# Attention and a routed MoE on one core: small VectorE operations taken out or handed to ScalarE, the first expert's weights loaded behind the second routing instead of from a guess

## The chip, the core and the metric

The kernel runs on one core of a Trainium2 chip. Its engines work side by side, each through a queue of its own: TensorE (PE; PEld is its weight load) does matmuls and transposes, VectorE (DVE) and ScalarE (ACT) move results out of PSUM and do elementwise work, GpSimd (POOL) issues gathers and scatters by index, SyncE (SP) issues the other DMAs. The metric is the device time of one execution in microseconds, the median of several runs.

## The reference, cut to what matters

```python
# q, k, v: (8 batches, 8 heads, 576, 64); p: (8, 8, 32, 64)
p_packed = sm_attn(p, k, v)             # 32 packed queries of each head attend to its 576 keys
out = sm_attn(q, p_packed, p_packed)    # 576 queries of each head attend to the 32 packed rows
x = out.transpose(0, 2, 1, 3).reshape(4608, 512)
...
logits = x @ w_gate + modality_bias[modality_id]     # 8 experts
e_idx = np.argmax(logits, axis=1)
gate_w = softmax(logits)[e_idx]
for e in range(8):
    out[e_idx == e] = gate_w * (np.maximum(x[e_idx == e] @ w1[e], 0) @ w2[e])   # 512 -> 1024 -> 512
```

With these inputs the argmax picks three experts only: expert 4 for 2311 rows, expert 5 for 1406, expert 7 for 891. Of the first quarter of the rows (the first routing) 569 go to expert 4 and 583 to expert 5; of the first half 1158, 841 and 305 go to experts 4, 5 and 7.

## The kernel before, in words

**Attention** is cut into eight units: a pair of batches (four pairs) and one of two groups of heads. A unit loads k, q and v, transposes them on TensorE (ScalarE copies `kT` out of PSUM, L218), and makes the scores of the packed queries. `scores1` finds the row maximum on VectorE (L239), turns it into the bias `nb` (L242), and ScalarE takes the exponential with that bias and the scale (L246). `a` and `p` steps multiply by v and give the packed rows; then `g`, `s` steps make the second softmax, on VectorE but for the exponential (L316 to L338, `a2T`). `x` steps (L354) multiply by the packed values: one matmul gives the outputs and, in extra columns, the gate logits. ScalarE copies the outputs to `xs` (L365), VectorE the logits to `lt` (L367); both read one PSUM tile of a pool of two, so that the next but one tile waits for both. `w` stores `xs` to the scratch in DRAM (SyncE, L379 and L380).

**The loop.** Units 0 to 5 run in one loop of a schedule written by hand: the string `ORDER` lists one period, in which each item is a step of the unit n, or of a later one (`>`). Each engine runs its instructions in the order in which they are issued there. An `e` issues the next piece of the extra work of a unit (`more`: a routing, or the split of W1), an `f` the next scatter (`spread`). The rest of units 6 and 7 follows the loop, and a scheduler mixes it with the first MoE slots.

**Routing.** After units 1, 3, 5 and 7 (`routing(i)`, from L417) VectorE computes from `lt` each row's expert, its rank and its gate weight. `scatter(i)` writes the rows' numbers into a list on DRAM: nine indirect DMAs by GpSimd (L469), each with a cast of its column of indices on VectorE ahead of it (L468). A table of **slots** is made from the counts by some 48 operations on tiles of 128x8 and less (`table_phase`, L577): table a, 2 slots, after the second routing; table b, 4 slots, after the third; table c, the rest, after the last. The argument behind the table's name is the expert that the phase starts with.

**A slot** takes 256 rows of one expert: gather (L662), transpose (L675), first matmul (L695; L714 for half slots), relu, second matmul (L730), scatter of the output (L735). The fp32 product is made of three fp32r ones, so W1 and W2 are split into a high part (ScalarE, L655) and a low part (VectorE, L656) at each change of expert. `load_w` (L644) brings 2 x 1024 KB of W1 or W2.

**The guess.** After the first routing `first_expert` (L535 to L545) finds the expert with most rows so far, SyncE reads it as `e0i`, and W1 of that expert is loaded. `split_first` splits it in the loop's last pieces. Table a starts with that expert; a branch at the first slot (L843) loads and splits W1 again if the table's first slot is of another.

Of the kernel before, what the change touches and what calls it, by code (L numbers as in the profile page):

```python
# [8 lines left out]
F32 = mybir.dt.float32  # L9
# [14 lines left out]
def packed_attn_moe_kernel(  # L24
# [14 lines left out]
    nc = tc.nc  # L39
# [127 lines left out]
    def prep_p(ps1, n4):  # L167
        t = ps1.tile([P, 512], F32, name="ps1")
        for n in range(4):
            nc.tensor.transpose(out=t[:, n * P:n * P + P], in_=pz[:, n4 + n].rearrange("p a d -> p (a d)"),  # L170
                                identity=ident)
        yield
        nc.vector.tensor_copy(out=pT[:, n4:n4 + 4, :], in_=t.rearrange("p (n c) -> p n c", n=4))
        yield
# [10 lines left out]
    def attention(i, g, lt, A, Z):  # L185
# [49 lines left out]
        def scores1(u):  # L235
            s1 = scores(ps2, pT[:, 2 * (2 * i + u) + g, :], D_["k"], u)
            yield
            mx = sm.tile([P, 1], F32, name="mx")
            nc.vector.tensor_reduce(mx, s1, axis=AX.X, op=ALU.max)  # L239
            yield  # L240
            nb = sm.tile([P, 1], F32, name="nb")
            nc.vector.tensor_scalar_mul(nb, mx, -SCALE)  # L242
# [4 lines left out]
                                 scale=SCALE, accum_out=r1[:, u])  # L247
# [94 lines left out]
        def xpart(c0):  # L342
# [24 lines left out]
            nc.vector.tensor_copy(out=lt[:, g, :, c0:c0 + w], in_=xq[:, :, :, P:XW])  # L367
# [24 lines left out]
        for nm, f, args in (("k", trans, [("k", *z) for z in fw]), ("q", trans, [("q", *z) for z in fw]),  # L392
# [3 lines left out]
            for n, z in enumerate(args or [()]):  # L396
# [4 lines left out]
    ORDER = ("<f >>c0 e >>>k4 >t >>>k2 s0 >>c0 >q4 >t >>>k4 >>>k3 e >>dv >q0 >>>k0 >>c0 s0 e >q0 f s0 >>>k2 >>r s0 >s1 "  # L401
# [15 lines left out]
    def routing(i, lt, ps1):  # L417
# [42 lines left out]
        dests[i] = dsf  # L460
# [4 lines left out]
    def scatter(i):  # L465
        for c in range(NC):
            dsi = sm.tile([P, 1], I32, name=f"dsi{c}", bufs=2)
            nc.vector.tensor_copy(out=dsi, in_=dests[i][:, c:c + 1])  # L468
            ins = ins_of(nc.gpsimd.indirect_dma_start(  # L469
                out=lst, out_offset=bass.IndirectOffsetOnAxis(ap=dsi, axis=0),  # L470
# [63 lines left out]

    def first_expert():  # L535
        cnt, mxc = st_("cnt"), st_("mxc", 1)
        tt(out=cnt, in0=base[1], in1=base0, op=ALU.subtract)
        nc.vector.tensor_reduce(mxc, cnt, axis=AX.X, op=ALU.max)
        nc.vector.scalar_tensor_tensor(out=cnt, in0=cnt, scalar=mxc, in1=desc[:, 0, :], op0=ALU.is_equal, op1=ALU.mult)
        e0 = const.tile([P, 1], F32, name="e0")  # L540
        nc.vector.tensor_reduce(e0, cnt, axis=AX.X, op=ALU.max)
        tsc(out=e0, in0=e0, scalar1=-1.0, scalar2=float(E), op0=ALU.mult, op1=ALU.add)
        e0i = const.tile([P, 1], I32, name="e0i")
        nc.vector.tensor_copy(out=e0i, in_=e0)
        return e0, e0i  # L545
# [195 lines left out]
    NU = 2 * NA[1]  # L741
    with ExitStack() as actx:
# [13 lines left out]
        def route(i):  # L756
            yield from routing(i, lts[i], ZL["ps1"])
            if i == 0:
                E0.extend(first_expert())
                E0.append(val(E0[1], 0, 0, (ET.SP,), 0, E - 1))  # L760
                load_w(W, 0, E0[2])
# [10 lines left out]
        def split_first():  # L772
            yield
            yield
            for z in range(4):
                split_w(W, 0, None, (z,))
                yield

        E0 = []
        more = {-1: rest(), NU - 1: split_first()}  # L780
# [5 lines left out]
        with tc.manual_schedule(engines={ET.PE, ET.DVE, ET.Activation, ET.SP}):  # L786
            for n in range(-6, NU + 6):
                for z in ORDER.split():
                    nm = z.lstrip("<>")
                    m = n + z.count(">") - z.count("<")  # L790
                    if nm in "ef":
                        next((more if nm == "e" else spread).get(m, iter(())), None)
# [17 lines left out]
    T = [table_phase("a", E0[0], NA[0], None, SA[0])]  # L810
    er = val(T[0]["tab"], 0, 1, (ET.SP,), 0, E - 1)
    load_w(W, 1, er)
# [24 lines left out]
    def sw(n, which, after=()):  # L837
# [4 lines left out]
        def go():  # L842
            if n == 0 and which == 0:  # L843
# [132 lines left out]
```

## Time and profile before

| | us |
|---|---|
| median of three runs | 632.21 |
| the three runs | 629.63, 632.21, 632.35 |
| the profiled execution: time | 628.84 |
| the profiled execution: span of the trace | 627.0 |
| TensorE busy in the span | 575.3 (92%) |
| VectorE, ScalarE, GpSimd busy | 251.3, 219.6, 148.3 |

The span is what the trace covers; the 1.8 us between the span and the execution's time lie around it. All rows below are of this one execution, which ran 3.4 us under the median. `xs` stores of units 0 to 5 are issued at 51.3, 65.1, 83.2, 99.6, 116.9 and 137.6 us; the loop's last `a2T` is done at 148.3; the first matmul of a slot starts at 162.2 and the last output scatter at 616.9.

### The profile page before, as it was taken

How to read it: one execution, taken by the hardware profiler on the slowest of the kernel's cores; microseconds unless marked ns; L12 is line 12 of the kernel's file. 1: busy time of each engine (PE TensorE's matmuls, PEld its weight loads, DVE VectorE, ACT ScalarE, POOL GpSimd, SP SyncE). 2: the span in 40 equal slices, each digit the busy share in tenths (PEclk: the TensorE clock that was granted, in tenths of full speed). 3: DMA queues.
4: the chain of work that ended last, by engine and by line, in shares of the span. 5: the costliest groups of instructions: out<-in, count | busy, mean ns of one | idle time of the engine just before them, and what ended most of it. 6: DMA issues, size and time to landing. Idle time of an engine off the chain costs nothing. (4 is left out here: it accounts for less than half of the span.)

```text
span 627.0 us, 12550 instructions
## 1 busy us (share of the span) xinstructions
PE 575.3 (92%) x4820; PEld 501.0 (80%) x4820; DVE 251.3 (40%) x669; ACT 219.6 (35%) x401; POOL 148.3 (24%) x183
## 2 busy tenths in 40 slices
PE   4979888875999999999999999999999999999982
PEld 4657666653889889899889889989989989989982
DVE  1469988987564421127120155012012012012281
ACT  3658676852432121126121154112112122122371
POOL 2020031352162142232203121312212112212221
PEclk9989999966899999999999999999999999999997
DMA  9899999939719311025902117211011011011112
GB/s 295 238 269 310 316 359 320 271 80 344 247 34 321 146 37 52 18 70 213 414 30 68 53 52 286 70 52 53 35 52 51 35 52 53 34 52 52 37 51 56
DMA packets 49226, 87.49 MB, mean 140 GB/s; under 512 B 12529, under 2 KB 22321, under 8 KB 49137
## 3 DMA queue, kind: packets, MB, share of 16 engines
q1 hardware_dynamic: 39024, 63.92, 31.9%
q0 software_dynamic: 8528, 22.16, 11.0%
q8 instruction: 49, 0.80, 0.5%
q10 hardware_dynamic: 1584, 0.28, 0.2%
q14 instruction: 41, 0.33, 0.2%
HBM read 66.78 MB, written 19.56 MB: 138 GB/s over the span
## 5 line engine op out<-in xcount | busy, mean ns | idle before, releaser
L695 PE MATMUL ps_h<-x_hl,w1h 128*128 128x256 f32 x1088 | 197.5, 283 | 0.7 <-ACTq L926 0.7
L695 PEld LDWEIGHTS ps_h<-x_hl,w1h 128*128 128x128 f32 x1088 | 170.9, 192 | 2.7 <-ACTq L926 0.9
L695 PE MATMUL ps_h<-x_hl,w1l 128*128 128x256 f32 x544 | 154.2, 283 | 0.0
L700 DVE SCALAR_TENSOR_TENSOR hl<-ps_h,hh 128x512 fp32r<-128x512 f32 x68 | 47.0, 691 | 256.2 <-ACT hh L699 253.8
L730 PE MATMUL ps_o<-w2h,hh 128*128 128x512 f32 x296 | 118.1, 399 | 2.8 <-ACT ot L734 2.0
L730 PE MATMUL ps_o<-w2h,hl 128*128 128x512 f32 x296 | 116.5, 393 | 0.0
L730 PE MATMUL ps_o<-w2l,hh 128*128 128x512 f32 x296 | 115.9, 392 | 0.2 <-DVEq L865 0.2
L695 PEld LDWEIGHTS ps_h<-x_hl,w1l 128*128 128x128 f32 x544 | 104.2, 192 | 0.6 <-issue 0.5
L699 ACT ACTIVATE hh<-ps_h 128x512 fp32r<-128x512 f32 x68 | 40.7, 598 | 160.7 <-PE ps_h L695 149.5
L735 POOL DMA_INDIRECT out_dram<-ot,mt x37 | 40.6, 1096 | 184.2 <-ACT ot L734 120.5
L734 ACT ACTIVATE ot<-ps_o,mt 128x512 f32<-128x512 f32 x37 | 25.4, 688 | 143.7 <-PE ps_o L730 120.0
L730 PEld LDWEIGHTS ps_o<-w2h,hh 128*128 128x128 f32 x296 | 55.7, 188 | 14.3 <-ACT ot L734 3.1
L469 POOL DMA_INDIRECT lst<-meta,dsi x36 | 37.1, 1031 | 126.4 <-DVE dsi L468 68.7
L730 PEld LDWEIGHTS ps_o<-w2h,hl 128*128 128x128 f32 x296 | 55.6, 188 | 11.5
L730 PEld LDWEIGHTS ps_o<-w2l,hh 128*128 128x128 f32 x296 | 55.7, 188 | 11.0 <-DVEq L865 0.6
L662 POOL DMA_INDIRECT xt<-x_scr,mt x46 | 45.0, 979 | 76.1 <-PE ps_t L675 29.7
L218 ACT COPY kT<-ps 128x512 f32<-128x512 f32 (+1 forms) x80 | 40.9, 553 | 21.1 <-PE ps L215 18.1
L354 PE MATMUL ps<-bd,a2T 64*128 64x136 f32 (+1 forms) x320 | 29.1, 339 | 9.8 <-DVE bf L523 4.3
L678 DVE TENSOR_TENSOR x_hl<-ps_t,x_hl 128x512 fp32r<-128x512 f32 x42 | 27.6, 684 | 19.7 <-ACTq L865 13.5
L354 PEld LDWEIGHTS ps<-bd,a2T 64*128 64x128 f32 (+1 forms) x320 | 22.0, 206 | 16.7 <-issue 8.3
L660 POOL DMA_DIRECT2D mt<-lst x23 | 17.3, 752 | 54.9 <-DMA out_dram<-ot,mt 44.4
L215 PE MATMUL ps<-ident,rek 128*128 128x128 f32 x144 | 22.4, 293 | 8.2 <-DMA rek<-in_k_dram 7.6
(187 smaller groups left out, 645.4 us busy)
## 6 DMA issues: line engine op xcount, KB each, us to landing
raw<-in_moe_w_dram SPq DMA_DIRECT2D x24, 1024.0 KB
rek<-in_k_dram SPq DMA_DIRECT2D x16, 576.0 KB
req<-in_q_dram SPq DMA_DIRECT2D x16, 576.0 KB
ld_v<-in_v_dram SPq DMA_DIRECT2D x16, 576.0 KB
x_scr<-xs SPq DMA_DIRECT2D x28, 256.0 KB
x_scr<-ld_v SPq DMA_DIRECT2D x4, 256.0 KB
x_scr<-xs SPq DMA_DIRECT2D x14, 64.0 KB
raw<-in_p_dram SPq DMA_DIRECT2D x2, 384.0 KB
```

Source lines behind the costliest of these rows:

```text
L215: nc.tensor.transpose(out=t[:, c * P:c * P + P], in_=src[:, (f0 + c) * P:(f0 + c) * P + P], identity=ident)
L218: nc.scalar.copy(out=T_[:, f0:f0 + w, :], in_=t[:, :w * P].rearrange("p (f r) -> p f r", f=w))
L354: nc.tensor.matmul(xp[rows, pr, z * XW:z * XW + XW], a2T[rs, t0:t0 + n], D_["bd"][rs, u, :], start=True, stop=True)
L469: ins = ins_of(nc.gpsimd.indirect_dma_start(out=lst, out_offset=bass.IndirectOffsetOnAxis(ap=dsi, axis=0), in_=meta[:, i * NC + c, :], in_ ...
L662: ins.append(nc.gpsimd.indirect_dma_start(out=xt[:, t], out_offset=None, in_=x_scr[0:NA[ph] * 2 * S] if ph < 2 else x_scr, in_offset=bass. ...
L678: iv = tt(out=M["xl"][:, :, ts], in0=ps, in1=M["xh"][:, :, ts].bitcast(F32), op=ALU.subtract)
L695: nc.tensor.matmul(ps[:, f], M[a][:, j, (f0 + f) * P:(f0 + f) * P + P], M[b][:, j], start=(n == 0), stop=(n == 3 * KD - 1))
L699: ia = nc.scalar.activation(out=M["hh"][:, fs], in_=ps, func=AF.Relu)
L700: iv = nc.vector.scalar_tensor_tensor(out=M["hl"][:, fs], in0=ps, scalar=0.0, in1=M["hh"][:, fs].bitcast(F32), op0=ALU.max, op1=ALU.subtract)
L730: nc.tensor.matmul(op, M[a][:, j, t * P:t * P + P], M[b][:, j, :], start=(n == 0), stop=(n == 3 * KF - 1))
L734: nc.scalar.activation(out=ot, in_=op, func=AF.Copy, scale=mt.bitcast(F32)[:, t, 2:3])
L735: nc.gpsimd.indirect_dma_start(out=out, out_offset=bass.IndirectOffsetOnAxis(ap=mt[:, t, 1:2], axis=0), in_=ot, in_offset=None, bounds_che ...
```

## The change

- `pT` is multiplied by the scale when it is copied out of PSUM; `scores1` takes the maximum with the sign turned and writes `nb` at once (16 operations of L242 go), and the exponential has no scale.
- The `lt` copies go from VectorE to ScalarE, right behind the `xs` copy of the same tile.
- The indices of a routing are cast at once, 9 columns, in `routing` (one operation for nine, L468 goes).
- `first_expert` goes, with the load of W1 after the first routing, and with the branch at the first slot. Table a is made within the loop, in one straight piece (`first_phase`, an `e` of unit 5), starting from expert 0; then W1 of the table's own first expert is loaded, and split late in the loop.
- `ORDER` is another string.
- Table b's code stands behind the rest of units 6 and 7; scatters of the loop depend by hand on the VectorE or ScalarE instruction issued just ahead of them.

```diff
-        nc.vector.tensor_copy(out=pT[:, n4:n4 + 4, :], in_=t.rearrange("p (n c) -> p n c", n=4))
+        nc.vector.tensor_scalar_mul(pT[:, n4:n4 + 4, :], t.rearrange("p (n c) -> p n c", n=4), SCALE)
...
-            mx = sm.tile([P, 1], F32, name="mx")
-            nc.vector.tensor_reduce(mx, s1, axis=AX.X, op=ALU.max)
-            yield
             nb = sm.tile([P, 1], F32, name="nb")
-            nc.vector.tensor_scalar_mul(nb, mx, -SCALE)
+            nc.vector.tensor_reduce(nb, s1, axis=AX.X, op=ALU.max, negate=True)
...
-                                 scale=SCALE, accum_out=r1[:, u])
+                                 accum_out=r1[:, u])
...
-            nc.vector.tensor_copy(out=lt[:, g, :, c0:c0 + w], in_=xq[:, :, :, P:XW])
+            nc.scalar.copy(out=lt[:, g, :, c0:c0 + w], in_=xq[:, :, :, P:XW])
...
-        dests[i] = dsf
+        dests[i] = sm.tile([P, NC], I32, name="dsi", bufs=2)
+        nc.vector.tensor_copy(out=dests[i], in_=dsf)
...
-            dsi = sm.tile([P, 1], I32, name=f"dsi{c}", bufs=2)
-            nc.vector.tensor_copy(out=dsi, in_=dests[i][:, c:c + 1])
...
-    def first_expert():
...
+    no_expert = const.tile([P, 1], F32, name="no_expert")
+    nc.vector.memset(no_expert, 0.0)
...
-            if i == 0:
-                E0.extend(first_expert())
-                E0.append(val(E0[1], 0, 0, (ET.SP,), 0, E - 1))
-                load_w(W, 0, E0[2])
...
-        def split_first():
-            yield
-            yield
-            for z in range(4):
-                split_w(W, 0, None, (z,))
-                yield
+        def first_phase():
+            T.append(table_phase("a", no_expert, NA[0], None, SA[0]))
+            yield
+            T[0]["er"] = val(T[0]["tab"], 0, 1, (ET.SP,), 0, E - 1)
+            load_w(W, 0, T[0]["er"])
+            yield
...
-    T = [table_phase("a", E0[0], NA[0], None, SA[0])]
-    er = val(T[0]["tab"], 0, 1, (ET.SP,), 0, E - 1)
-    load_w(W, 1, er)
+    load_w(W, 1, T[0]["er"])
...
-            if n == 0 and which == 0:
-                with tc.If(val(tb, s, 3, IFE, 0, 1) > 0):
-                    load_w(W, 0, val(tb, s, 1, (ET.SP,), 0, E - 1))
-                    split_w(W, 0)
-            else:
-                with ExitStack() as es:
-                    for z in after if n == 0 else ():
-                        es.enter_context(tc.issue_after(z))
-                    split_w(W, which)
+            with ExitStack() as es:
+                for z in after if n == 0 else ():
+                    es.enter_context(tc.issue_after(z))
+                split_w(W, which)
```

**VectorE, table a, before.** The table's operations are dealt out among those of the second softmax (`m`, `st`, `dn`; `ps_1853` is a tile of an `x` step).

```order
L319 TENSOR_REDUCE m_1889<-st 128x18
L551 TENSOR_TENSOR ex_m<-eidx,ex_s 128x8
L566 TENSOR_TENSOR row<-row_e,ex_s 128x8
L568 TENSOR_REDUCE tab_f<-ex_s 128x1
L504 TENSOR_TENSOR dot<-starts,ex_s 128x8
L504 TENSOR_TENSOR dot<-ends,ex_s 128x8
L552 TENSOR_REDUCE tab_f<-ex_m 128x1
L567 TENSOR_REDUCE tab_f<-row 128x1
L499 TENSOR_REDUCE red<-dot 128x1 x2
L367 COPY lt<-ps_1853 128x2x24
L321 TENSOR_TENSOR st<-st,m_1889 128x576
L326 TENSOR_REDUCE dn<-st 128x18
```

**VectorE, table a, after.** It is one piece (the first 12 of its 48 rows), in which most rows read what the row ahead wrote.

```order
L563 TENSOR_TENSOR cnt<-run_84,base_80 128x8
L487 TENSOR_SCALAR tl_f<-cnt 128x8
L488 CAST tl_i<-tl_f 128x8
L489 TENSOR_SCALAR tl_i<-tl_i 128x8
L490 CAST tl_o<-tl_i 128x8
L570 TENSOR_SCALAR cl<-cnt 128x8
L582 MEMSET tab_f 128x1
L509 TENSOR_SCALAR key<-eidx,no_expert 128x8
L582 MEMSET tab_f 128x1
L510 TENSOR_SCALAR key_m<-key 128x8
L511 TENSOR_TENSOR key<-key,key_m 128x8
L517 TENSOR_TENSOR bf<-key 128x64
```

The table has moved out of the softmax of the loop's last units and stands between two softmax pieces.

**SyncE, the load of W1, before.** `raw_114` is W1 as loaded; it stands after the first routing, ahead of the loads of k and q (`rek`, `req`) of later units.

```order
L207 DMA ld_v<-in_v_dram 64x4x576 x2
L631 TENSOR_LOAD e0i
L644 ISA
L644 DMA raw_114<-in_moe_w_dram 128x2x1024
L644 ISA
L644 DMA raw_114<-in_moe_w_dram 128x2x1024
L195 DMA rek<-in_k_dram 128x2x576 x2
L195 DMA req<-in_q_dram 128x2x576 x2
```

**SyncE, after.** The same two loads stand behind those of the last q and ahead of unit 4's `xs` stores; SyncE reads the expert from `tab_a` first.

```order
L207 DMA ld_v<-in_v_dram 64x4x576 x2
L195 DMA req<-in_q_dram 128x2x576 x2
L615 TENSOR_LOAD tab_a
L628 ISA
L628 DMA raw_114<-in_moe_w_dram 128x2x1024
L628 ISA
L628 DMA raw_114<-in_moe_w_dram 128x2x1024
L376 DMA x_scr<-xs 64x4x256 x2
L377 DMA x_scr<-xs 64x256
```

The load has moved past the k, q and v loads of the loop, and past the stores of units 2 and 3, and now waits for table a.

**VectorE behind the loop, before.** Three `lt` copies stand among the end of table b and the next key; `lt<-ps_2471` is the first.

```order
L557 CAST tab_b<-tab_f 128x7
L513 TENSOR_SCALAR key<-eidx,last_b 128x8
L605 SCALAR_TENSOR_TENSOR pref<-pref,tab_f 1x1
L608 CAST pre_b<-pref 1x1
L367 COPY lt<-ps_2471 128x2x24
L514 TENSOR_SCALAR key_m<-key 128x8
L515 TENSOR_TENSOR key<-key,key_m 128x8
L521 TENSOR_TENSOR bf<-key 128x64
L367 COPY lt<-ps_2487 128x2x24
```

**ScalarE behind the loop, after.** The same three copies, each right behind the `xs` copy of its tile.

```order
L362 COPY xs<-ps_2297 128x2x3x128
L364 COPY lt<-ps_2297 128x2x24
L362 COPY xs<-ps_2313 128x2x3x128
L364 COPY lt<-ps_2313 128x2x24
L661 CAST x_hl<-ps_t_2287 128x4x128
L362 COPY xs<-ps_2334 128x2x3x128
L364 COPY lt<-ps_2334 128x2x24
L661 CAST x_hl<-ps_t_2287 128x4x128
L639 CAST w2h<-raw_2236 128x1024 x4
```

The copies left VectorE's queue, where table b stands ahead of them, for ScalarE's.

## Rows read from the trace of the kernel before

**Rows 1.** Busy us by stretch: length, five engines (named in the row), TensorE clock, DMA share, GB/s.
```profile
core 0: us, PE busy (x) PEld busy (x) DVE busy (x) ACT busy (x) POOL busy (x), PEclk, DMA share, GB/s
51.55:65.33 13.78, 13.78 (x242) 10.80 (x240) 12.26 (x31) 11.26 (x24) 0.00 (x0) 1.00 1.06 323
65.33:83.44 18.11, 15.14 (x247) 11.27 (x245) 16.92 (x60) 11.90 (x26) 3.36 (x3) 1.00 1.05 320
83.44:99.92 16.48, 14.61 (x240) 11.01 (x239) 12.77 (x37) 11.16 (x25) 5.76 (x6) 1.00 1.06 351
99.92:121.95 22.03, 19.74 (x324) 14.41 (x323) 21.76 (x101) 16.09 (x35) 5.06 (x5) 1.00 1.03 311
121.95:148.40 26.45, 14.70 (x178) 10.35 (x179) 24.33 (x82) 13.48 (x26) 11.60 (x11) 0.74 0.59 159
148.40:162.20 13.80, 11.56 (x121) 9.16 (x121) 8.19 (x48) 6.82 (x9) 0.00 (x0) 0.51 0.98 361
162.20:616.00 453.80, 448.01 (x2969) 404.73 (x2965) 130.42 (x252) 121.01 (x202) 113.19 (x116) 1.00 0.27 91
```

**Rows 2.** Timeline of SyncE's DMA issues: start us, us, engine, line, operation.
```profile
51.33 1.28 SPq L379 DMA_DIRECT2D x_scr<-xs  x2
...
77.59 0.97 SPq L644 DMA_DIRECT2D raw<-in_moe_w_dram  x2
...
99.55 1.27 SPq L379 DMA_DIRECT2D x_scr<-xs  x2
```

**Rows 3.** Groups of instructions by line, 0 to 165 us: busy, mean ns, idle before.
```profile
L239 DVE TENSOR_REDUCE mx<-ps 128x1 f32<-128x576 f32 x16 | 12.0, 749 | 1.0 <-PE ps L229 1.0
...
L656 DVE TENSOR_TENSOR w1l<-raw,w1h 128x1024 fp32r<-128x1024 f32 x4 | 4.9, 1219 | 0.1
...
L367 DVE COPY lt<-ps 128x48 f32<-128x48 f32 x21 | 4.2, 202 | 8.8 <-ACT xs L365 8.8
L655 ACT CAST w1h<-raw 128x1024 fp32r<-128x1024 f32 x4 | 4.1, 1046 | 0.0
...
L468 DVE CAST dsi<-dsf 128x1 int32<-128x1 f32 x27 | 3.1, 134 | 0.0
...
L242 DVE TENSOR_SCALAR nb<-mx 128x1 f32<-128x1 f32 x16 | 2.2, 139 | 0.1
```

**Rows 4.** Timeline of VectorE: first and last of six operations of `first_expert`.
```profile
75.73 0.11 DVE L537 TENSOR_TENSOR cnt<-run,base 128x8 f32<-128x8 f32 x1
...
76.71 0.15 DVE L544 CAST e0i<-e 128x1 int32<-128x1 f32 x1
```

**Rows 5.** Timeline of VectorE: four of its rows from 108 to 122 us.
```profile
108.63 0.16 DVE L579 TENSOR_TENSOR cnt<-run,base 128x8 f32<-128x8 f32 x1
...
116.50 0.15 DVE L551 TENSOR_TENSOR ex_m<-eidx,ex_s 128x8 f32<-128x8 f32 x1
...
117.14 0.19 DVE L367 COPY lt<-ps 128x48 f32<-128x48 f32 x1
...
121.51 0.15 DVE L557 CAST tab_a<-tab_f 128x7 int32<-128x7 f32 x1
```

**Rows 6.** Timeline of all engines behind the loop.
```profile
148.40 1.73 PE L354 MATMUL ps<-bd,a2T 64*128 64x136 f32 x12 [4.34 <-DVE bf L523]
...
150.22 0.80 ACT L365 COPY xs<-ps 128x768 f32<-128x768 f32 x1 [4.09 <-PE ps L354]
...
151.94 0.18 DVE L367 COPY lt<-ps 128x48 f32<-128x48 f32 x1
...
152.18 2.23 PE L354 MATMUL ps<-bd,a2T 64*128 64x136 f32 x16 [2.04 <-DVE lt L367]
```

**Rows 7.** Waits of TensorE, 162 to 627 us: us in total, times, longest.
```profile
PE ps_h L714 <- DVE w1l L656: 1.7, 1, 1.7
...
PE ps_h L695 <- ACTq L926: 0.7, 1, 0.7
```

**Rows 8.** Timeline of TensorE at 127 us.
```profile
127.34 0.44 PE L292 MATMUL ps<-ident,pd 128*128 128x128 f32 x2 [3.47 <-DVE dsi L468]
```

More of the change, by code (lines that the diff above doesn't have):

```diff
@@ L398, in attention @@
         return steps
-    ORDER = ("<f >>c0 e >>>k4 >t >>>k2 s0 >>c0 >q4 >t >>>k4 >>>k3 e >>dv >q0 >>>k0 >>c0 s0 e >q0 f s0 >>>k2 >>r s0 >s1 "
[3 rows of a table removed]
+    ORDER = (">>c0 >p >q2 s1 >>>k4 >t >>c0 s0 >>>k3 >q3 >>>k2 >t s1 >s0 >>>k4 f >s0 >>c0 >>>k1 x0 >s0 >q3 >>>k2 f >g "
[3 rows of a table added]
     def run_all(u, order):
@@ L466, in scatter @@
         for c in range(NC):
-            dsi = sm.tile([P, 1], I32, name=f"dsi{c}", bufs=2)
-            nc.vector.tensor_copy(out=dsi, in_=dests[i][:, c:c + 1])
             ins = ins_of(nc.gpsimd.indirect_dma_start(
-                out=lst, out_offset=bass.IndirectOffsetOnAxis(ap=dsi, axis=0),
+                out=lst, out_offset=bass.IndirectOffsetOnAxis(ap=dests[i][:, c:c + 1], axis=0),
                 in_=meta[:, i * NC + c, :], in_offset=None))
@@ L533, in sel_at @@
         return o
-    def first_expert():
[L536 to L545, printed above, removed]
     def expert_at(starts, ends, v, out_):
@@ L741, in packed_attn_moe_kernel @@
     NU = 2 * NA[1]
+    T = []
+    no_expert = const.tile([P, 1], F32, name="no_expert")
+    nc.vector.memset(no_expert, 0.0)
     with ExitStack() as actx:
@@ L770, in rest @@
             yield
-        def split_first():
+        def first_phase():
+            T.append(table_phase("a", no_expert, NA[0], None, SA[0]))
             yield
+            T[0]["er"] = val(T[0]["tab"], 0, 1, (ET.SP,), 0, E - 1)
+            load_w(W, 0, T[0]["er"])
             yield
-            for z in range(4):
-                split_w(W, 0, None, (z,))
-                yield
-        E0 = []
-        more = {-1: rest(), NU - 1: split_first()}
+        more = {-1: rest(), NU - 1: first_phase()}
         spread = {}
@@ L790, in packed_attn_moe_kernel @@
                     m = n + z.count(">") - z.count("<")
-                    if nm in "ef":
-                        next((more if nm == "e" else spread).get(m, iter(())), None)
+                    if nm == "e":
+                        next(more.get(m, iter(())), None)
+                    elif nm == "f":
+                        ins = next(spread.get(m, iter(())), None)
+                        if ins is not None:
+                            at = next(z for z in reversed(nc.cur_bb.bb.instructions) if z.engine in (ET.DVE, ET.Activation))
+                            tc.add_manual_dep(ins, at.name, SYNC, reason="scatters with time between them")
                     elif 0 <= m < NU or (m == NU and nm[0] not in "xw") or (m == NU + 1 and nm[0] in "dkcq"):
@@ L882, in packed_attn_moe_kernel @@
         Z1.update(ps1=ZL["ps1"], ps2=ZL["ps2"], xs=ZL["xs"])
-        T.append(table_phase("b", T[0]["last"], NA[1], T[0]["used"], SA[1] - SA[0]))
         ZL["st"] = (lp, zq)
@@ L888, in packed_attn_moe_kernel @@
         run_all(u, "x0 x1 x2 w")
+        T.append(table_phase("b", T[0]["last"], NA[1], T[0]["used"], SA[1] - SA[0]))
         for _ in routing(NA[1], lts[NA[1]], ZL["ps1"]):
```

6 rows, old and new, of the table ORDER are left out of this document.

## The prediction, made before the changed kernel had run

> **What bounds the kernel now.** I read the busy time by stretch first, with the bounds set where unit after unit stores its `xs`. TensorE has 448.01 of the slots' 453.80 us [rows 1]: there it is the bound, with 5.8 us to win at most. So the change has to earn its time ahead of 162 us, in three places that differ.
>
> The stretches of units 0 to 3 (51.55 to 99.92, 48.4 us): the first is all TensorE, 13.78 of 13.78; the second and third issue as many matmuls (242, 247, 240) and take 18.11 and 16.48 [rows 1]. Two things stand over them. The DMA share is above 1 in all three, at 320 to 351 GB/s: the queue of loads is never empty. And in the second VectorE is busy for 16.92 of 18.11. W1's 2 x 1024 KB are issued at 77.59, inside it [rows 2].
>
> The tail of the loop (99.92 to 148.40, 48.5 us): VectorE is busy 21.76 + 24.33 = 46.1 of it, TensorE 34.4 [rows 1]. VectorE is the bound: TensorE waits for it, for example 3.47 us ahead of 127.34 [rows 8]. In the last part the granted clock is .74 on average, and .51 in the 13.8 us behind the loop: TensorE had work for 14.70 of the 26.45 us, the clock fell to the lower of its two levels, 1.2 GHz, for about half of them, and the 11.56 busy us behind the loop run nearly all at that level.
>
> **The change, part by part.** The sum is made against the profiled 628.84.
>
> *Loop, units 0 to 3.* `first_expert` is a chain: its six timed operations start at 75.73 to 76.71 [rows 4], five steps of .196 us where each operation needs the one before it. With the last one's step it held VectorE for 1.05 us in a stretch where that engine is nearly full: −1.1, and 17.0 for the second stretch. The load of W1, 2.1 MB, leaves a queue that is always busy: at 351 to 320 GB/s that is 6.0 to 6.6 us of transfer which the loads behind it no longer wait for. How much of it TensorE gets is unknown. Nothing at one end; at the other all three stretches fall to the first one's 13.78, 41.3 us, which is −7 for both effects. The third stretch has 16.48 − 14.61 = 1.9 us without TensorE; I take 1.4 of it, since steps of VectorE that TensorE waits for stay. Sum of the part: −2.5 (0 to −7).
>
> *Loop, tail.* What VectorE loses: an `lt` copy, 202 ns long [rows 3], between a step of .07 and .20; I take .13, nine times, −1.2. Sixteen of 18 casts of indices: a small operation among others takes a step of .07 (nine, counting the double one as two, between 116.50 and 117.14 [rows 5]; their own 134 ns overlap [rows 3]): −1.1. Four `nb` at .07: −.3. Together −2.6. The maximum with its sign turned I cost as the 749 ns it takes now [rows 3]; no row shows a turned sign, and the same pass over 576 elements is the nearest. The `lt` copies cost ScalarE some .2 each, which lies beside its busy share of 51 to 73% there (16.09 of 22.03, 13.48 of 26.45 [rows 1]); bare, nine would be 1.8.
>
> What VectorE gains is dearer. Table a, dealt out before between 108.63 and 121.51 [rows 5], is one block of 48 rows, of which I count 33 that read what the row ahead wrote. Interleaved, 48 × .07 = 3.4. Straight, 33 × .196 + 15 × .07 = 7.5. So +4.1, and as VectorE bounds the tail, all of it is on the path. The routing's chain loses its partners too: eight of its operations stood among the table's, 8 × (.196 − .07) = +1.0. Then W1: SyncE reads the expert from the finished table, and the load takes 6.0 to 6.6 us beside its .97 of issue [rows 2]. `xs` stores of unit 4 wait behind it on SyncE. ScalarE's `w1h` (4 × 1046 ns) and VectorE's `w1l` (4 × 1219 ns [rows 3]) stand in their queues behind softmax work of the last unit, about 8 us of VectorE by the rows behind the block; I take a wait of 0 for them, at most 2. If it came, everything behind on ScalarE, the last unit's exponentials first, would be late. Part: −2.6 + 4.1 + 1.0 = +2.5 (−2.6, the savings alone, to +7, dependent steps everywhere and the wait).
>
> On dependent operations the Trainium skill speaks against my largest term. "VectorE: DVE Perf Modes", section "The DRAIN you can't avoid", says that a next operation starts only when the pipe is empty, and that a semaphore between operations costs nothing extra; dependent rows would then cost no more than others. By that the block costs +0 and the sum is 4.1 lower. The trace has .07 against .196 per step and does not agree.
>
> *Behind the loop.* TensorE's second `x` tile starts at 152.18, after 2.04 us without work, released by the `lt` copy at 151.94 [rows 6]. ScalarE's copy of `xs` from 150.22 took .80, so it was done at 151.02; the `lt` copy came .92 later because table b stands ahead of it on VectorE. On ScalarE it follows at once. −1.0 (0 to −1.5); the clock does not matter for a wait. Table b itself must still be ready for its slots, which start some 2 slots, over 40 us, later.
>
> *Slots.* Table a starts with expert 0 as its "expert so far", not with a guess; of the three that occur the first is then expert 4 instead of 5 (the largest of the first quarter, 583 rows against 569, so that the guess held and no reload ran). The number of slots stays 20, 17 full and three halves. Before, the last two were halves with a change of expert between, and TensorE waits 1.7 us there for `w1l` [rows 7]. A half gives half the time to hide a split. Now halves are followed by a full slot of another expert twice, as once before, which cost .7 [rows 7], and there is no change ahead of the last slot: −1.7 + .7 = −1.0 (0 to −2). The branch that goes costs a few register instructions before the first slot; I take nothing, as `w2h` was still being cast there.
>
> *Sum.* −2.5 + 2.5 − 1.0 − 1.0 = −2.0, so 626.8 for an execution like the profiled. That one ran 3.4 under the median of the three; the median is what is measured: 632.2 − 2.0 = **630.2**. Half a per cent, 3.2 us, is about what a measurement here can tell from no change: 629.05 and 635.4 are the bounds.
>
> **The rivals.**
>
> *The loop falls to TensorE's floor.* If the loads are what holds the second and third stretch, they go from my 45.9 to 41.3: 4.6 more, 625.6. For it speaks the DMA share above 1; against it that TensorE is not busy to the brim where VectorE is.
>
> *The table's block is no dearer than before.* If dependent rows step as interleaved ones do, the 4.1 is not lost: 626.1. That is what the page named above makes of it. Against it stand the steps of .196.
>
> *Slower: the block starves TensorE and its clock.* While VectorE works through routing and table, both PSUM tiles of the pool of two that the softmax scores use are held; TensorE soon runs out of other work. It idles some 6 us, and the low clock, now granted for part of the last stretch, comes for all of it. The 14.70 us of work at a mean of .74 would take 14.70 × .74 / .5 = 21.8: +7.1, of which the idle time hides up to half: +3.5 to +7.1. With the middle, 5.5, 635.7. It decides when TensorE's idle time in the block exceeds the 3.47 seen now [rows 8]. For it: VectorE has no slack at 46.1 of 48.5. Against: in the new order TensorE has transposes of q to do beside it.
>
> *Nothing is gained in the loop.* ScalarE's `lt` copy may come as late as VectorE's did, and W1 may not have held anyone: without the −2.5 the time is 632.7.
>
> **How the numbers follow.** Forecast .45, its own range 627 to 634, and .13 of it under 629.05. Floor .17 (625.6), block for nothing .09 (626.1), slower .19 (635.7 and above), nothing gained .10 (632.7). Faster: .13 + .17 + .09 = .39. Slower .19. The rest, .42, within half a per cent. The range that leaves out 2 in 10 reaches from 622.5, where floor and a cheap block partly join, to 638, with the slower case's upper end.
>
> **What would show it.** Units' stores: the third after the first (51.33 to 99.55 now [rows 2]) should be 2 to 3 us nearer. The block of 48 table rows on VectorE should take 7 to 8 us, not 3 to 4. No cast of indices should stand among the softmax. TensorE's longest wait in the tail should stay under some 4 us, and the clock's mean near .74. `w1h` should not wait for its load. Behind the loop TensorE should wait for ScalarE's `lt` about 1 us less, and in the slots the single wait of 1.7 should be gone. The prediction is wrong if the last stretch of the loop grows by more than 3 us (clock or W1's landing), or if units 0 to 3 come down to 41 us.

## The result, and the profile after

The changed kernel takes 639.85 us (median of four runs, 638.91 to 641.43) against 631.22 for the kernel before beside it: a ratio of 1.0141, 95% interval 1.0106 to 1.0176. It is slower by 8.6 us, where 2.0 less was forecast. The profiled execution took 640.36, with a span of 638.8.

Busy time by stretch of the changed kernel, with the bounds set at the same events as in [rows 1]: the `xs` stores of units 0, 1, 2, 3 and 5, then the first matmul of a slot.

```profile
core 0: us, PE busy (x) PEld busy (x) DVE busy (x) ACT busy (x) POOL busy (x), PEclk, DMA share, GB/s
54.48:68.96 14.48, 14.48 (x241) 10.04 (x240) 11.83 (x26) 11.56 (x28) 0.00 (x0) 1.00 1.03 300
68.96:87.90 18.94, 16.44 (x244) 11.12 (x243) 15.35 (x41) 11.80 (x29) 4.78 (x5) 0.91 1.04 322
87.90:108.00 20.10, 17.99 (x241) 11.83 (x240) 12.12 (x26) 11.67 (x28) 4.66 (x5) 0.92 0.96 262
108.00:151.34 43.34, 31.38 (x461) 20.59 (x459) 37.62 (x123) 25.24 (x55) 10.72 (x11) 0.84 0.66 183
151.34:173.25 21.91, 16.04 (x155) 12.59 (x151) 16.96 (x83) 11.13 (x22) 5.96 (x5) 0.62 0.98 319
173.25:628.00 454.75, 447.63 (x2969) 404.80 (x2965) 122.46 (x234) 116.31 (x199) 112.18 (x116) 1.00 0.25 84
```

Units 0 to 3 now take 53.5 us (54.48 to 108.00) instead of 48.4. The first two stretches are .7 and .8 longer; the third is 20.10 for 16.48, with the same number of matmuls (241 for 240) and less than 12.2 us of work on each of VectorE and ScalarE. TensorE's time without work is about the same in it (2.1 for 1.9); it counts as busy for 3.4 us more, at a granted clock of .92 for 1.00. From unit 3's stores to the first slot matmul it is 65.3 us; it was 62.3. The slots did not move.

**The third stretch.** Timeline of the changed kernel in it, all engines, some rows left out.

```profile
90.91 0.96 POOL L465 DMA_INDIRECT lst<-meta,dsi  x1 [0.40 <-issue]
...
91.03 0.95 PE L270 MATMUL ps<-ld_v,a1T 64*64 64x128 f32 x11
...
92.17 0.96 POOL L465 DMA_INDIRECT lst<-meta,dsi  x1 [0.30 <-ACT st L320]
...
92.31 0.45 PE L270 MATMUL ps<-ld_v,a1T 64*64 64x128 f32 x3 [0.33 <-issue]
...
93.44 0.95 POOL L465 DMA_INDIRECT lst<-meta,dsi  x1 [0.30 <-issue]
...
94.83 0.42 PE L270 MATMUL ps<-ld_v,a1T 64*64 64x128 f32 x3 [0.52 <-issue]
...
95.67 0.37 ACT L218 COPY kT<-ps 128x256 f32<-128x256 f32 x1 [3.68 <-remote]
```

TensorE does the last matmuls of a step of 24 mostly three at a time, with gaps "<-issue": it waits for nothing that the profile shows. ScalarE stands still for 3.68 us, released by "remote", an event that the records don't place. All of it lies beside four scatters of the list that GpSimd issues in a row: one at 89.29, and the three shown, 1.6 us behind it and then 1.3 us apart. Before, each scatter had its own cast on VectorE ahead of it [rows 3]. Right behind this crawl the granted clock is low, .60 and .54 from 96 to 100 us.

**The tail.** Timeline of the changed kernel from the table's first row to the split of W1.

```profile
127.48 0.16 DVE L563 TENSOR_TENSOR cnt<-run,base 128x8 f32<-128x8 f32 x1
...
130.00 0.17 DVE L522 TENSOR_TENSOR ends<-starts,tl_o 128x8 f32<-128x8 f32 x1
130.20 0.23 DVE L527 TENSOR_SCALAR sel_g<-ends,sidx 128x8 f32<-128x8 f32 x1
...
135.63 0.16 DVE L541 CAST tab_a<-tab_f 128x7 int32<-128x7 f32 x1
135.71 0.75 DVE L239 TENSOR_REDUCE nb<-ps 128x1 f32<-128x576 f32 x1
...
136.51 0.97 SPq L628 DMA_DIRECT2D raw<-in_moe_w_dram  x2
136.55 0.74 ACT L243 ACTIVATE a<-ps,nb 128x576 f32<-128x576 f32 x1 [6.60 <-DVE nb L239]
...
137.43 1.29 PE L229 MATMUL ps<-kT,pT 64*32 64x320 f32 x16 [5.70 <-ACT a L243]
...
144.98 3.89 ACT L639 CAST w1h<-raw 128x1024 fp32r<-128x1024 f32 x4 [3.39 <-DMA raw<-in_moe_w_dram]
...
148.03 1.25 PE L351 MATMUL ps<-bd,a2T 64*128 64x136 f32 x8 [3.42 <-DVE st L313]
```

Table a's 48 rows fill VectorE from 127.48 to 135.71, 8.2 us. The row maximum `nb` stands behind them; ScalarE's exponential waits 6.60 for it, TensorE 5.70. Then the load of W1, issued at 136.51, is there at 144.98: ScalarE, whose next instruction is the split, waits 3.39 for it, and TensorE 3.42 behind that. The granted clock over 108.00 to 151.34 is .84, and .62 up to the first slot.

**Behind the loop**, the `lt` copy follows its `xs` copy at once.

```profile
163.89 0.80 ACT L362 COPY xs<-ps 128x768 f32<-128x768 f32 x1 [3.65 <-PE ps L351]
...
164.59 0.20 ACT L364 COPY lt<-ps 128x48 f32<-128x48 f32 x1
...
164.84 2.24 PE L351 MATMUL ps<-bd,a2T 64*128 64x136 f32 x16 [1.04 <-ACT lt L364]
```

TensorE waits 1.04 there, where it waited 2.04 [rows 6].

**In the slots**, waits of TensorE (us in total, times, longest).

```profile
PE ps L289 <- DVE pd L282: 1.7, 1, 1.7
```

The wait of 1.7 for `w1l` is gone [rows 7]. There are two of up to .8 at changes of expert, and the line shown: for `pd` of unit 7 it was .2 before and is 1.7.

### The profile page after: what moved, and what is told of

It reads as the page before. It is cut to its first block, busy times and chain, and to the rows that moved or that the text cites. A ratio compares the mean times of both kernels' runs of the same rounds, so it can differ in the third digit from the quotient of the medians.

```text
span 638.8 us, 12452 instructions
## 1 busy us (share of the span) xinstructions
PE 583.8 (91%) x4820; PEld 498.4 (78%) x4820; DVE 240.0 (38%) x584; ACT 214.7 (34%) x417; POOL 146.8 (23%) x183
## 5 line engine op out<-in xcount | busy, mean ns | idle before, releaser
L215 PEld LDWEIGHTS ps<-ident,rek 128*128 128x128 f32 x144 | 17.8, 157 | 18.7 <-issue 16.0
L215 PE MATMUL ps<-ident,rek 128*128 128x128 f32 x144 | 25.5, 310 | 7.2 <-DMA rek<-in_k_dram 7.2
```

Source lines behind the costliest of these rows:

```text
L215: nc.tensor.transpose(out=t[:, c * P:c * P + P], in_=src[:, (f0 + c) * P:(f0 + c) * P + P], identity=ident)
```

## The experiments

Runs are compared by their ratio to the kernel before, run beside each, and by the stretches of their profiles: "units 0-3" from unit 0's stores to unit 3's, "tail" from there to unit 5's, "behind" to the first slot matmul, "slots" to the last output scatter. What one kernel costs over another is the difference of their ratios times 631 us, because the kernel before was itself up to 1.6 us apart between the groups of runs; such a difference is known to some 2 to 4 us. Times come from the timelines; one profile each, so differences of 1 to 2 us in a single stretch say little (e3 and e13 are the same kernel, and 2.4 apart in units 0 to 3). No median was taken of those marked 1.

| kernel | median us | ratio, 95% interval | units 0-3 | tail | behind | slots |
|---|---|---|---|---|---|---|
| before | 631.2 | 1 | 48.2 | 38.1 | 24.6 | 454.7 |
| changed | 639.9 | 1.0141 (1.0106 to 1.0176) | 53.5 | 43.3 | 22.1 | 454.9 |
| e1 old order | 636.3 | 1.0083 (1.0042 to 1.0125) | 48.5 | 44.3 | 22.5 | 454.7 |
| e2 guess back | 642.8 | 1.0178 (1.0151 to 1.0204) | 55.4 | 44.0 | 21.0 | 456.3 |
| e3 lt alone | 631.4 | 1.0001 (0.9984 to 1.0017) | 48.7 | 39.0 | 22.1 | 455.7 |
| e4 small edits, scatters free | 653.8 | 1.0355 (1.0298 to 1.0412) | 58.4 | 49.2 | 24.5 | 454.9 |
| e5 old order, guess | 629.7 | 0.9992 (0.9970 to 1.0013) | 46.5 | 38.4 | 21.2 | 455.9 |
| e6 small edits, scatters tied | 631.0 | 1.0017 (0.9999 to 1.0035) | 46.7 | 38.0 | 23.0 | 456.3 |
| e7 nine casts | 635.5 | 1.0094 (1.0060 to 1.0128) | 46.7 | 44.5 | 22.4 | 454.9 |
| e8 W1 by number | 642.8 | 1.0206 (1.0174 to 1.0239) | 59.6 | 38.8 | 21.3 | 454.9 |
| e9 block alone | 634.5 | 1.0084 (1.0053 to 1.0116) | 46.7 | 43.9 | 22.4 | 455.4 |
| e10 late W1 alone | 637.4 | 1.0109 (1.0074 to 1.0144) | 45.9 | 47.7 | 22.3 | 456.2 |
| e11 new order, guess, nine casts | 640.1 | 1.0151 (1.0099 to 1.0203) | 52.6 | 40.5 | 20.9 | 456.7 |
| e12 before again | 629.1 (1) | | 48.3 | 38.1 | 24.6 | 454.7 |
| e13 lt alone again | 627.3 (1) | | 46.3 | 38.7 | 21.3 | 456.2 |
| e14 table b late | 627.7 (1) | | 47.7 | 38.1 | 24.5 | 454.7 |

**First theories.** One: the new order costs, most of it in units 0 to 3. The rival: the table's block, with W1 behind it, costs, all of it in the tail.

**e1, old order.**

```diff
-    ORDER = (">>c0 >p >q2 s1 >>>k4 >t >>c0 s0 ...
+    ORDER = ("<f >>c0 e >>>k4 >t >>>k2 s0 >q4 ...
```

> The changed kernel with the order of the loop of before (less the two items of the operation that is gone); table a and the load of W1 stay where the changed kernel has them. If the new order is what costs (TensorE's idle time and slower matmuls in units 0 to 3, 7 to 8 us by the stores of unit 3: 107.8 after, 99.6 before), the time falls from 639.9 to about 633 and unit 3's stores are issued at about 100 us. If the table's block and W1's late load cost (the tail), it stays at 637 to 640, with unit 3's stores early and the tail longer.

It came out between the two: unit 3's stores at 102.0, the loop as before, and a tail 6.2 longer than before. So both seem to have a part: some 3.7 us go with the order, some 5.2 stay.

**e2, guess back.**

```diff
+                E0.extend(first_expert())
+                E0.append(val(E0[1], 0, 0, (ET.SP,), 0, E - 1))
+                load_w(W, 0, E0[2])
...
-            T.append(table_phase("a", no_expert, NA[0], None, SA[0]))
```

> The changed kernel with the guess back: first_expert and the early load of W1 after the first routing, table a outside the hand-written loop, the branch at the first slot; the new order stays. If the table's block with W1 behind it costs, the tail shortens by 5 to 8 us and the time is 632 to 634. If the new order costs, unit 3's stores stay at 108 us or later (the load of W1 comes back into the queue) and the time is 637 to 640. The order of the experts is that of before again: if it was worth something, the slots take as long as before, otherwise as after.

Neither theory held: it is no faster than the changed kernel (the intervals overlap). The new order with the early W1 has the highest median of the four corners (e5 is the fourth). In its profile VectorE waits 3.2 and ScalarE 3.0 us for "remote", until 152.69 and 154.21, beside four gathers (L658) that GpSimd issues in a row from 148.36 to 152.22. The kernel before issues the same four in a row and has no such wait:

```profile
139.23 1.02 POOL L662 DMA_INDIRECT xt<-x_scr,mt  x1 [0.68 <-DMA mt<-lst]
...
143.10 1.11 POOL L662 DMA_INDIRECT xt<-x_scr,mt  x1 [0.30 <-issue]
```

**e3, lt copies alone.**

```diff
-            nc.vector.tensor_copy(out=lt[:, g, :, c0:c0 + w], in_=xq[:, :, :, P:XW])
+            nc.scalar.copy(out=lt[:, g, :, c0:c0 + w], in_=xq[:, :, :, P:XW])
```

> The kernel before with the lt copies on ScalarE and nothing else. By the prediction's terms: 1.0 less behind the loop and about 1.2 less on VectorE in the tail, so 629 against 631.2. If the copies only change engines, or delay ScalarE's exponentials, 631 to 632.

No change in the time that can be told. In the profile 2.5 us are gained behind the loop, and 1.0 is given back in the slots.

**e4, small edits, scatters free.** The kernel before, with the scale in `pT`, the maximum with its sign turned and one cast of indices for nine; the main lines:

```diff
-            nc.vector.tensor_reduce(mx, s1, axis=AX.X, op=ALU.max)
-            nc.vector.tensor_scalar_mul(nb, mx, -SCALE)
+            nc.vector.tensor_reduce(nb, s1, axis=AX.X, op=ALU.max, negate=True)
...
-            dsi = sm.tile([P, 1], I32, name=f"dsi{c}", bufs=2)
-            nc.vector.tensor_copy(out=dsi, in_=dests[i][:, c:c + 1])
...
-        dests[i] = dsf
+        dests[i] = sm.tile([P, NC], I32, name="dsi", bufs=2)
+        nc.vector.tensor_copy(out=dests[i], in_=dsf)
```

> The kernel before with the maximum that turns the sign (no nb operation, the scale in pT) and one cast of indices for nine, nothing else. By the prediction's terms 1.4 less in the tail: 629.8. If VectorE's small operations hide under others, no change: 631.

22.4 us slower by the ratio, with less work on VectorE. Timeline of this kernel at its second routing's scatters, and its busy time in two of the 2 us stretches there.

```profile
124.63 1.21 POOL L465 DMA_INDIRECT lst<-meta,dsi  x1 [33.07 <-DVE dsi L458]
...
125.45 0.76 PE L303 MATMUL ps<-wgs,ppT 64*32 64x8 f32 x16
...
126.15 0.96 POOL L465 DMA_INDIRECT lst<-meta,dsi  x1 [0.31 <-issue]
...
126.69 0.49 PE L257 MATMUL ps<-ident,a 128*128 128x128 f32 x3 [0.48 <-issue]
...
127.41 0.96 POOL L465 DMA_INDIRECT lst<-meta,dsi  x1 [0.30 <-issue]
...
135.01 0.96 POOL L465 DMA_INDIRECT lst<-meta,dsi  x1 [0.31 <-issue]
136.21 0.17 ACT L306 COPY bd<-ps 128x16 f32<-128x16 f32 x1 [10.43 <-remote]
...
136.43 2.84 PE L351 MATMUL ps<-bd,a2T 64*128 64x136 f32 x24 [8.61 <-ACT bd L306]
```

```profile
core 0: us, PE busy (x) PEld busy (x) DVE busy (x) ACT busy (x) POOL busy (x), PEclk, DMA share, GB/s
...
132.00:134.00 2.00, 0.00 (x0) 0.00 (x0) 0.00 (x0) 0.00 (x0) 1.39 (x3) 0.50 0.02 4
134.00:136.00 2.00, 0.00 (x0) 0.00 (x0) 0.00 (x0) 0.00 (x0) 1.67 (x2) 0.50 0.04 8
```

Nine scatters run in a row, one each 1.27 us, the first two 1.5 (three of them shown, and the last). Beside the second and third TensorE thins out, then TensorE, VectorE and ScalarE stop. ScalarE's copy at 136.21 reads matmuls that TensorE started at 125.45; it starts .2 us after the last scatter's issue ends (135.01 + .96 = 135.97). At 132 to 136 the DMA share is .02 to .04: there the stop doesn't come from transfers that fill the DMA engines. The first routing's nine scatters do the same at 82 to 93 us, with a DMA share near 1. Whether the engines lacked instructions was not tested; no packet of an instruction queue is on record from 127.8 to 141.0, so none came where they went on.

This made a new theory: scatters in a row stop the other engines, and in the kernel before the casts that the change took from VectorE kept them apart.

**e6, the same with the scatters tied** as in the changed kernel:

```diff
+                        ins = next(spread.get(m, iter(())), None)
+                        if ins is not None:
+                            at = next(z for z in reversed(nc.cur_bb.bb.instructions) if z.engine in (ET.DVE, ET.Activation))
+                            tc.add_manual_dep(ins, at.name, SYNC, reason="scatters with time between them")
```

> The kernel before with the small VectorE operations gone, as in the run that took 653.8, but with each scatter of the loop tied to the VectorE or ScalarE instruction issued just ahead of it, as in the changed kernel. If the 23 us came from scatters that ran back to back once their casts no longer spaced them, the time falls to 630 to 634. If it is the turned-sign maximum or the scale in pT, it stays at 650 or above.

The 22 us are gone. The ties are the one difference between e4 and e6, so nine scatters that may run in a row cost this kernel 21 us (1.0355 against 1.0017). The turned-sign maximum costs what the plain one did (751 ns against 749 [rows 3]).

**e7, nine casts** in the changed kernel:

```diff
-        dests[i] = sm.tile([P, NC], I32, name="dsi", bufs=2)
-        nc.vector.tensor_copy(out=dests[i], in_=dsf)
+        dests[i] = dsf
...
+            dsi = sm.tile([P, 1], I32, name=f"dsi{c}", bufs=2)
+            nc.vector.tensor_copy(out=dsi, in_=dests[i][:, c:c + 1])
```

> The changed kernel with nine casts of indices on VectorE again, one ahead of each scatter. If four scatters in a row at 89 to 94 us cost the changed kernel its crawl (3.7 us of ScalarE without work, TensorE three matmuls at a time), unit 2's to unit 3's stores come down from 20.1 to 16 to 17 us and the time to 636. If spacing is as good with the ties, 640 or above, for the nine casts' own 1.1 us.

By the ratios 3.0 us come back (4.4 by the medians), about as much as the two intervals can tell apart; in the profile it is all in units 0 to 3. Busy time of this kernel from unit 1's stores to unit 2's and to unit 3's, and its last four scatters of the first routing:

```profile
core 0: us, PE busy (x) PEld busy (x) DVE busy (x) ACT busy (x) POOL busy (x), PEclk, DMA share, GB/s
...
68.45:85.82 17.37, 14.83 (x241) 9.98 (x240) 14.91 (x45) 11.56 (x28) 4.10 (x4) 1.00 1.05 328
85.82:100.63 14.81, 14.81 (x243) 10.37 (x244) 12.58 (x31) 11.85 (x28) 5.07 (x5) 1.00 0.94 238
```

```profile
87.72 1.23 POOL L466 DMA_INDIRECT lst<-meta,dsi  x1 [0.88 <-DVE dsi L465]
...
89.25 0.96 POOL L466 DMA_INDIRECT lst<-meta,dsi  x1 [0.30 <-issue]
...
90.52 0.96 POOL L466 DMA_INDIRECT lst<-meta,dsi  x1 [0.31 <-DVE dn L325]
...
90.69 0.89 PE L270 MATMUL ps<-ld_v,a1T 64*64 64x128 f32 x24
...
91.78 0.96 POOL L466 DMA_INDIRECT lst<-meta,dsi  x1 [0.30 <-issue]
```

The third stretch is all TensorE now, 14.81 of 14.81, against 17.99 of 20.10; its clock is 1.00 again (.92), and the 24 matmuls of a step run in .89 us. But the casts did not do it by spacing: these four scatters stand 1.5 and 1.3 us apart, as close as the four of the changed kernel, and nothing stops beside them. So the crawl is there with one cast and gone with nine, and four scatters in a row are not enough to make it; what is stays open. The second stretch, 17.37 for 18.94, is no part of this: in both profiles TensorE waits 2.2 us in it for VectorE's `pd`, and only in the changed kernel's is the granted clock low behind that wait (.50 from 80 to 82 us).

**e5, the fourth corner:** the changed kernel's small edits, with the `ORDER` of e1 and the guess of e2.

> The fourth corner: the changed kernel's small edits (lt on ScalarE, no nb operation, one cast of indices, tied scatters, table b late) with the old order and the guess (early W1, table a outside the hand-written loop). From unit 0's stores to the first slot matmul: 110.9 us before, 119.0 after, 115.3 with the old order alone, 120.4 with the guess alone back. If the new order and the table in the loop are the two costs and the small edits cost nothing, this span is 109 to 111 and the time 629 to 631; if untied casts or the scatters cost here too, 112 to 116 and 633 to 637.

As fast as before, and no faster that can be told: with the old order the small edits cost nothing and give nothing, once the scatters are tied and the table is dealt out.

**e9, the block alone:** e5, with table a made in one piece inside the loop.

```diff
         def split_first():
+            T.append(table_phase("a", E0[0], NA[0], None, SA[0]))
             yield
...
-    T.append(table_phase("a", E0[0], NA[0], None, SA[0]))
```

> The kernel with the old order, the guess and the small edits (629.7, as before), and table a made in one straight piece inside the loop, starting from the guess; W1 comes early as before. It has the block alone of what the old order with the table and the late W1 had (636.3). If the block costs what its steps do (8.2 us against 3.4 dealt out) and TensorE waits 5 us beside it, the time is 633 to 635. If the wait for W1 was the cost, 629 to 631.

5.8 us over e5 (4.8 by the medians). Its timeline, the block's first and last row and TensorE behind it:

```profile
118.47 0.16 DVE L575 TENSOR_TENSOR cnt<-run,base 128x8 f32<-128x8 f32 x1
...
126.76 0.16 DVE L553 CAST tab_a<-tab_f 128x7 int32<-128x7 f32 x1
...
128.56 1.29 PE L229 MATMUL ps<-kT,pT 64*32 64x320 f32 x16 [5.77 <-ACT a L243]
```

The tail is 43.9, as in the changed kernel, with W1 loaded early. Against e1 (the block and the late W1) it is 1.0084 to 1.0083: the late W1 added nothing that can be told on top of the block. From unit 3's stores to the first slot matmul e9 takes 66.2 us for e5's 59.6; TensorE is without work for 4.9 of the 6.7 us more, and busy for 1.8 more with the same matmuls, at a mean clock of .77 for .80.

**e10, the late W1 alone:** e5, with W1 of the guess loaded where the changed kernel loads it, and split late and in one piece.

```diff
-                load_w(W, 0, E0[2])
...
         def split_first():
             yield
+            load_w(W, 0, E0[2])
+            yield
+            yield
+            yield
+            yield
+            yield
+            split_w(W, 0)
             yield
-            for z in range(4):
-                split_w(W, 0, None, (z,))
-                yield
```

> The same kernel, without the block, and with W1 of the guess loaded late: in SyncE's queue where the changed kernel has it, ahead of the last v loads, and split behind the last exponential of the last unit's first softmax. It has the late load alone. If W1's landing holds ScalarE and VectorE in the tail, the time is 632 to 635. If the block is the cost, 629 to 631, or 1 less for the load that left the k, q and v queue.

7.4 us over e5. Its timeline, the issue of the load and the split:

```profile
123.89 1.57 SPq L640 DMA_DIRECT2D raw<-in_moe_w_dram  x2
...
136.22 3.88 ACT L651 CAST w1h<-raw 128x1024 fp32r<-128x1024 f32 x4 [8.81 <-DMA raw<-in_moe_w_dram]
```

ScalarE stood 8.81 us before its split, 12.3 us after the issue of the load. So the two costs don't add: the block alone costs 5.8, the late load alone 7.4, both together 5.7 (e1). It fits that without the block the loop reaches the split sooner, while the load takes its time, so that the block hides the load. Units 0 to 3 lost only .6 against e5 when the load left their queue, which one profile each can't tell from nothing.

**e8, W1 by number.**

```diff
+            if i == 0:
+                load_w(W, 0, 4)
...
-            load_w(W, 0, T[0]["er"])
```

> The changed kernel with W1 of expert 4, by number, loaded after the first routing; the table stays in the loop. It knows the answer ahead, to take away the wait for the table and the load alone. If W1's landing costs the tail (ScalarE waits 3.4 us for it ahead of its casts, TensorE 3.4 behind that), unit 5's stores come 3 to 5 us sooner after unit 3's and the time is 635 to 637, less what the load costs among k, q and v. If the table's block is the cost (TensorE 5.7 us idle beside it), 639 to 640.

It can't be read as meant. The scheduler moved the split up right behind the load:

```profile
75.15 2.77 SPq L628 DMA_DIRECT2D raw<-in_moe_w_dram  x2
...
85.78 1.04 ACT L639 CAST w1h<-raw 128x1024 fp32r<-128x1024 f32 x1 [11.68 <-DMA raw<-in_moe_w_dram]
```

ScalarE waits 11.68 us for W1 in units 0 to 3 (59.6), which covers what it asked. Its tail, 38.8, holds the block, but neither a wait for W1 nor the split, whose `w1l` alone is 4.8 us of VectorE.

**e11, new order, guess and nine casts.**

> The changed kernel with the guess back (642.8) and nine casts that space the scatters. If the new order costs only through scatters in a row, this is 629 to 632, 11 us less, and nothing is wrong with the order itself. If the order has a cost of its own, 636 to 640.

1.7 us less than e2 by the ratios, which the intervals don't tell from none, and still 10.0 over e5. No "remote" wait is left, though its four gathers stand in a row as in e2. So with the early W1 the new order has a cost of its own; with the table in the loop it has none that shows (e7 1.0094, e1 1.0083).

**The start.** Unit 0's stores were at 51.3 us in the profile of before, and at 53.5 to 55.8 in the profiles of e1 to e11.

**e12, before once more.**

> The kernel before, unchanged, profiled a second time. Its first profile issued unit 0's stores at 51.3 us, all later profiles of kernels with the same start at 53.5 to 55.8. If the first was a quick one, this one shows 53 to 56 and 108 to 111 us from there to the first slot matmul. If the kernels' edits slowed the start, it shows 51 to 52.

51.5: no quick one. **e13 and e14** settle it: e3 again, unchanged, and the kernel before with one line moved.

```diff
-        T.append(table_phase("b", T[0]["last"], NA[1], T[0]["used"], SA[1] - SA[0]))
...
         run_all(u, "x0 x1 x2 w")
+        T.append(table_phase("b", T[0]["last"], NA[1], T[0]["used"], SA[1] - SA[0]))
```

> The kernel before with the lt copies on ScalarE, profiled a second time; in its first profile unit 0's stores came at 55.8 us, against 51.3 and 51.5 in the two of before, though none of its first 45 us is edited. If the start is a matter of the execution, it shows 51 to 54 now. If it belongs to the program, 55 to 56.

> The kernel before with table b's code behind the rest of units 6 and 7, the one part of the change not yet run alone; nothing ahead of the loop's end is edited. If the start differs by program even without an edit there, unit 0's stores are at 53 to 56; if only by execution or by edits, at 51 to 52. Behind the loop the wait for the lt copy (2.0 us of TensorE) should shrink by the 0.9 that table b took ahead of it, if the code's place decides VectorE's order there.

e13 has 53.0 where the same kernel had 55.8, and e14 has 50.8. So executions of one kernel differ there by some 3 us; the profiles' starts are not used for any cause. Whether some programs start later on the mean stays open. In e14 the place of table b's code hardly matters; TensorE's wait behind the loop is 1.86 for 2.04:

```profile
149.08 0.80 ACT L365 COPY xs<-ps 128x768 f32<-128x768 f32 x1 [4.10 <-PE ps L354]
...
150.62 0.19 DVE L367 COPY lt<-ps 128x48 f32<-128x48 f32 x1
...
150.87 2.24 PE L354 MATMUL ps<-bd,a2T 64*128 64x136 f32 x16 [1.86 <-DVE pre_b L608]
```

The copy on VectorE still starts .7 us after `xs` is done (149.08 + .80 = 149.88), behind table b's last rows.

## Why the prediction was wrong

**The step that failed first** is "sixteen of 18 casts of indices ... −1.1". They were priced as work of 70 ns each that goes, and nothing was put down for what they held apart; the scatters were read as GpSimd's own, off the path, and no rival named them. e4 and e6, with the ties as their one difference, show that scatters free to run nine in a row cost 21 us. In the changed kernel, which has ties, nine casts take away the crawl and some 3.0 us (e7), in the stretch where −1.4 was forecast. That much is measured; by what way the casts do it there is not known, since e7's scatters stand as close.

**The second step** is the tail, +2.5 (−2.6 + 4.1 + 1.0). It was +5.3. The block itself was well priced, 8.2 us for 7.5, a step of .17 us on average; the sum took its difference to 3.4, +4.1, and e9 measures 5.8 for the block. The −2.6 rested on "as VectorE bounds the tail, all of it is on the path", and none of it shows: with the small operations gone and the table dealt out the tail is 38.4 (e5) and 38.0 (e6), for 38.1 before. VectorE's full queue did not make each of its operations a cost; one piece of 8.2 us ahead of `nb` did.

**The slower rival**, given .19, had the number: 635.7, and e9 is at 634.5, e1 at 636.3. It had half of the mechanism. TensorE's wait beside the block is 5.70 in the changed kernel and 5.77 in e9, over 3.47, as its sign asked (e5 too has one wait of 4.3 for `pd`, and costs nothing, so the sign alone is not sharp). But its price came from the clock, 7.1 us by a low level throughout the last stretch, and that did not happen: from unit 3's stores to the first slot matmul the mean granted clock is .77 for .78 before, and in e9 idle time is 4.9 of the 6.7 us over e5. So that the number fits is in part luck.

**Loop, units 0 to 3: −2.5.** It was +5.3 (53.5 against 48.2). Without the crawl it is −1.6 (e7, 46.65 against 48.2), but e5 and e6, which keep `first_expert` and the early load, are at −1.7 and −1.5, and the same kernel gave 48.7 and 46.3 (e3, e13). So nothing shows of the part given to W1's transfer and to `first_expert`; the rival that nothing is gained in the loop fits better. The DMA share above 1 was read as a sign that loads hold TensorE. The rival of TensorE's floor was right only for the third stretch of e7, all TensorE, with 14.81 and not 13.78.

On dependent operations the Trainium skill, "VectorE: DVE Perf Modes", section "The DRAIN you can't avoid", says of eight copies that a semaphore after each cost nothing extra. The prediction carried this over to small operations that read what the one ahead wrote, and for them the measurement decides: in the block a row that does so starts .20 us behind the one ahead (130.00 to 130.20), one that doesn't .08 (135.63 to 135.71), and 48 rows took 8.23 us. The same section adds that a next operation that is not held starts earlier, and the trace agrees in so far as the row at 135.71 starts before the .16 us of the one at 135.63 are over.

**W1's landing: 0, at most 2.** It was 3.39 on ScalarE. The load was there 8.5 us after its issue, not 6.0 to 6.6 and .97, and the cover was looked for on VectorE while ScalarE's split, the first to need W1, had none. In the time it made little difference (e9 and e1), since the block was ahead of it; without the block it costs 7.4 (e10).

**lt on ScalarE: −1.0 behind the loop.** Right: the wait is 1.04 for 2.04. But e3 shows no change of the whole that can be told: the first slot starts sooner, and meets unit 7's `pd` behind the 4.6 us of `w2l` on VectorE: a wait of 1.6 us (e5) where there was .2.

**Slots: −1.0.** Right in size: 454.7 to 454.9 for kernels that start with expert 4 (changed, e1, e7, e8), 455.4 to 456.7 for those with lt on ScalarE and the old order of experts (e2, e3, e5, e9, e10, e11, e13). It pays for the `pd` wait, which e6 has too (1.5, slots 456.3), with lt still on VectorE. Behind the loop and slots together are at −2.3, where −2.0 was forecast.

**The sum.** By the ratios the changed kernel is 8.9 us slower. The casts are 3.0 of it (e7) and the block 5.8 (e9), with which the rest of the change comes out at +.1, less than these runs tell apart. No kernel here beats the one before; e5 equals it.

**Open.** How scatters in a row stop the others was not found, nor what in the changed kernel brings the crawl that e7 doesn't have: the records say "issue" and "remote", and what e4 excludes is transfers that fill the DMA engines. Why the new order costs 10 us with the early W1 (e11 against e5) wasn't followed up, as the changed kernel has no early W1.

## What to carry to other kernels

An instruction that another engine waits for may be what paces that engine: before taking it away, ask what runs closer together without it, and look at the timeline for the queue that it fed. The table's small dependent operations were nearly free here when dealt out among other work, and taking small ones away gave nothing back; in one piece they cost some .17 us each, and what counts is which engine's next instruction stands behind the piece. A busy share of 95% says that an engine may bound a stretch, not that each of its operations is on the path. The sign that would show a rival right (here TensorE's wait beside the table) should be worked out before its chance is set: VectorE's queue already said that `nb` stood behind the table.

## What the runs showed of the hardware

Nine indirect DMAs issued by GpSimd in a row, 1.27 us apart, went with the other engines slowing and then standing still, ScalarE for 10.4 and 10.7 us (e4, 653.8 us); with the scatters tied to other work it is gone (e6, 631.0). It ends .2 us after the last one's issue ends in the one case (136.21), 1.3 in the other (92.86 after 91.56), and in the first it goes on with the DMA engines nearly idle. Four in a row give no clear picture: ScalarE stands 3.7 us beside four scatters in the changed kernel and 3.0 beside four gathers in e2, but there is no such wait beside e7's four scatters, 1.5 and 1.3 us apart, nor beside the four gathers, 1.3 us apart, of the kernel before (139.23 to 143.10) and of e6 (140.12 to 144.07). So the number in a row and the distance don't decide by themselves.
